# Backward pass of a recurrent-memory attention layer on one core: output gradients by head in column groups, row sums in 32 bit in column groups, turns of 128 columns

## The chip, the cores and the metric

The kernel runs on one core of a Trainium2 chip. The metric is the device time of one execution in microseconds (us), as the median of several runs. A core has TensorE (PE; its loads of the stationary operand are shown as PEld), VectorE (DVE), ScalarE (ACT), GpSimd (POOL) and SyncE (SP), which work beside each other and wait for one another by semaphores. SP and POOL also issue the transfers (DMA). Matmul results lie in PSUM, eight banks of 128 partitions x 512 numbers of 32 bit; operands lie in SBUF.

## The reference

Forward and backward pass of a block: layer norm, attention with a recurrent memory, residual, layer norm, gated feed-forward, residual. S = 2048 rows of D = 448, H = 16 heads of 256, segments of 32 rows, a memory of M = 8 rows. For segment s:

```python
xs = x[:, s * seg_len:(s + 1) * seg_len, :].copy()
h = jnp.concatenate([mem, xs], axis=1)
q = jnp.einsum('btd,dhe->bhte', h, Wq)
...
p = _softmax(scores, axis=-1)
o = jnp.einsum('bhqk,bhke->bhqe', p, v)
o = jnp.einsum('bhte,hed->btd', o, Wo)
mem = o[:, :M, :].copy()
outs.append(o[:, M:, :])
```

The results are the output and, by jax.vjp, the gradients of x, of mem0 and of the seven weights. Since the memory of a segment is the first eight output rows of the segment before it, the 64 segments are a chain: forward from 0 to 63, backward from 63 to 0. A segment works on L = 40 rows, 8 of memory and 32 own ones.

## The kernel before, in words

The program has four stages: `forward_chain` (64 segments), `ffn_phase`, `backward_chain` (64 segments, in tiles of four: tile t = s // 4, place r = s % 4, from r = 3 down to 0) and `tail_phase` (the gradients of the weights, as matmuls over all rows). The kernel is written with a tile scheduler: it orders each engine's instructions by a priority and by its own model of when they are ready, and sets the semaphores. What stands in `with k.prio.crit()` has the highest priority, in the order of the program; `tc.issue_after(ins)` places an instruction behind another of the same engine. Everything outside, such as a tile's closing work, fills gaps. A tile of a pool that is used under one name with few buffers has to wait until the one before it has been read.

A segment of `backward_chain` before the change:

- **Output gradient by weights (L1236).** The gradient of the 40 output rows (`do_roll`: the 32 own rows, and the 8 memory rows that segment s+1 has just written) is multiplied with the output weights: 32 head pieces of 128 x 4 pieces of D, each with 128 x 128 weights as the stationary operand and 40 columns moving. The result, features on partitions, goes to `doT` in four copies.
- **Turns (L1245)** of `doT` in 16 matmuls to rows on partitions (`dO_sb`).
- **Scores (L1254)**: 32 small matmuls with the values give the gradient of the softmax's input, `pD`; DVE makes the score gradient `dS_bd` of it in four operations (L1261 to L1267).
- **Heads (L1213)**: gradients of values (from `dO_sb` and P), of keys (from q and dS) and of queries (from k and the turned dS, L1304). Each set is copied out in own rows (`blk`) and first, memory rows (`lo`), by L75 on DVE and L76 on ACT, the helper `evac`.
- **Rows (L1293)**: 96 matmuls, with 32 columns of `blk` stationary and 448 columns of the turned weights moving. They go to four groups of 32 columns of the array, j % 4, and so to four groups of 32 partitions of one bank, `pH`; the four partial sums still have to be added.
- **Sum and turn (L1319, L1322, L1326)**: `pH` is copied in 32 bit to `om`; four 32-bit matmuls with `om` stationary and `sel` moving (32 columns, which add the four groups) give the sum already turned, features on partitions; DVE copies 8 of its columns to `do_roll` for segment s-1. That closes the chain.
- The own rows' part is kept for the tile (L1334 to L1344), as the gradient of the normed x, turned.

At r = 0 the tile's memory rows are put through the same weights, 96 matmuls (L1378), summed and turned (L1385), turned back in 32 bit (L1393), and the layer norm's backward (`ln_bwd`, L249) writes 128 rows of the gradient of x. This stands outside `crit`.

Queues: SP issues per segment the turned load of the values (L1153, a transfer that transposes) and eight loads of q and k (L1163); per tile the turned load of the output gradient (L1147) and three loads for the norm (L1347, L1349). POOL issues the load of P (L1166) and the stores, and copies in SBUF. Each of these targets has one buffer, so a load waits for its last reader.

The forward chain works on the way from x to q and k in another form, which matters for the prediction: 32 rows stationary, 512 columns of weights moving, in four column groups (L569, and L576 with 64 rows of partitions), then turns of 128 columns (L593).

Of the kernel before, what the change touches and what calls it, by code (L numbers as in the profile page):

```python
# [145 lines left out]
def run_all(k: _K):  # L146
# [15 lines left out]
    psum = ctx.enter_context(tc.tile_pool(name="psum", bufs=1, space=bass.MemoryType.PSUM))  # L162
# [41 lines left out]
    def dt(name, shape, dtype=BF16):  # L204
# [7 lines left out]
              X_o=dt("X_o", [NB, P, MC * P]), HC=dt("HC", [NB * P, DP]), Oh=dt("Oh", [S, D]),  # L212
              DC0=dt("DC0", [P, 4, D]), DC1=dt("DC1", [P, NB - 4, D]))
# [18 lines left out]
    ffn_phase(k, lambda: next(back, None))  # L232
    for _ in back:
        pass
# [3 lines left out]
def cj(j):  # L238
    return (j % 2) * 16 + j // 2
# [869 lines left out]
def backward_chain(k: _K):  # L1109
# [7 lines left out]
    NWIN = 8  # L1117

    WoT_sb = W(0, KC, HD)
# [4 lines left out]
    lo_b = {"v": [A(40, 32, 32), A(42, 32, 32)], "k": [A(44, 32, 32), A(46, 32, 32)], "q": [B(5, 32, 32)]}  # L1124
    dxT = B(7, 1024).bitcast(FP32).rearrange("p (c n) -> p c n", n=P)
    vT = A(49.5, 16, 2 * L)
    dO_sb = A(52, 16, P)
    doT = A(56, 32, 64)
    do_roll = A(60, KC, NWIN, L)
    xn_t = B(9, D)  # L1130
    dh_h = [B(9.875, 448).bitcast(FP32), A(48.5, 448).bitcast(FP32)]
    dx3 = A(48, KC * 48).bitcast(FP32).rearrange("p (c n) -> p c n", c=KC)
    lq3 = k.mv2[:].rearrange("p t n -> p (t n)").bitcast(BF16).rearrange("p (c m) -> p c m", m=M)
    dx2 = [(A(64.5, 96).bitcast(FP32).rearrange("p (c n) -> p c n", c=2), 0, 2, P, 2),
           (A(48.375, 48).bitcast(FP32).rearrange("p (c n) -> p c n", c=1), 2, 3, P, 2),
           (k.maskb[:, 0:24].unsqueeze(1), 3, 4, 64, 2)]
    dx1 = B(4.375, KC * 48).bitcast(FP32).rearrange("p (c n) -> p c n", c=KC)
    dx_stage = [(dx3, 0, KC, P, 3)] + dx2 + [(dx1, 0, KC, P, 1)]
    dhx = A(62.5, KC, P)
    dmr = A(63.5, KC, 16, M)  # L1140
    P_bd, dS_bd, dST_bd = [B(1.25 * i, 8, 2, L) for i in range(3)]
    Pb = [B(3.75, 8, L)]

    def prep_tile(t):
        if t < 0:
            return
        nc.sync.dma_start_transpose(out=dhx, in_=dr["DHb"][t * P:(t + 1) * P, :])  # L1147
        s0 = (4 * t) % NWIN
        for kc in range(KC):
            nc.gpsimd.tensor_copy(out=do_roll[:, kc, s0:s0 + 4, 0:SEG], in_=dhx[:, kc, :].rearrange("p (g j) -> p g j", g=4))  # L1150
# [4 lines left out]
    def load_seg(s):  # L1155
        if s < NSEG - 1:
            load_v(s)
# [6 lines left out]
        P_sb = Pb[0]  # L1164
# [22 lines left out]
    load_seg(NSEG - 1)  # L1187
# [3 lines left out]
    nc.sync.dma_start(out=WoT_sb[:, 0:3, :], in_=dr["To"][:, 0:3, :])  # L1191
    nc.sync.dma_start(out=WoT_sb[0:64, 3, :], in_=dr["To"][0:64, 3, :])
    nc.gpsimd.memset(WoT_sb[64:P, 3, :], 0.0)
# [5 lines left out]
    nc.vector.memset(doT[:, :, L:64], 0.0)  # L1199
    nc.gpsimd.memset(dST_bd, 0.0)  # L1200
    nc.gpsimd.memset(dxT[:, KC - 1, :], 0.0)
    om = k.f32("f1", DP, "omb")
    nc.gpsimd.memset(om[:], 0.0)
# [5 lines left out]
    def head_mm(ps, lhs, rhs_bd, turned):  # L1209
        for cl in range(16):  # L1210
            b, i = divmod(cl, 6)
            at = 8 * (cl // 4 % 2) + 4 * (cl // 8) + cl % 4 if turned else cl
            nc.tensor.matmul(ps[b][:, i * 2 * L:(i + 1) * 2 * L], lhsT=lhs[:, at, :],  # L1213
                             rhs=rhs_bd[:, cl // 2, :, :].rearrange("p g n -> p (g n)"), start=True, stop=True)

    for s in range(NSEG - 1, -1, -1):
# [6 lines left out]
        P_sb = Pb[0]  # L1223
        if r == 2:
            prep_tile(t - 1)
        if s < NSEG - 1:
            load_seg(s)

        with k.prio.crit():
            pss = [k.ps1() for _ in range(4)]  # L1230
            for j in range(MC):
                c = cj(j)
                b, jj = divmod(j, 8)
                for kc in range(KC):
                    with tc.issue_after(k.last_dh.ins) if s == NSEG - 1 and j == 0 and kc == 0 else nullcontext():
                        nc.tensor.matmul(pss[b][:, jj * L:(jj + 1) * L], lhsT=WoT_sb[:, kc, c * P:(c + 1) * P],  # L1236
                                         rhs=do_roll[:, kc, sl, :], start=(kc == 0), stop=(kc == KC - 1))
            for b in range(4):
                k.evac(doT[:, 8 * b:8 * b + 8, 0:L], pss[b][:, 0:8 * L].rearrange("p (c n) -> p c n", n=L), "vsvs"[b])

            def token_major(hf):
                ph = k.ps1()[:].bitcast(BF16)
                for i in range(8):
                    c0 = 2 * (8 * hf + i)
                    nc.tensor.transpose(ph[:, i * P:(i + 1) * P], doT[:, c0:c0 + 2, :].rearrange("p c n -> p (c n)"), ident[:, :])  # L1245
                k.evac(dO_sb[:, 8 * hf:8 * hf + 8, :], ph.rearrange("p (c n) -> p c n", n=P), "sv"[hf])
            token_major(0)
            token_major(1)
            pD = k.ps1()
            for h in range(8):  # L1250
                for g in range(2):
                    for dc in range(DC):
                        j = 2 * (2 * h + dc) + g
                        nc.tensor.matmul(pD[64 * g:64 * g + 64, h * L:(h + 1) * L], lhsT=doT[:, j, :], rhs=vT[:, 2 * h + dc, L * g:L * g + L],  # L1254
                                         start=(dc == 0), stop=(dc == DC - 1), skip_group_check=True)
            if s == 0:
                k.tl.grads(0)
                k.tl.outs(4, 7, 0, 6)
            pD3 = pD[:, 0:8 * L].rearrange("p (h n) -> p h n", n=L)
            prod = k.f32("f2", 8 * L, "prod")[:].rearrange("p (h n) -> p h n", n=L)  # L1260
# [5 lines left out]
            def score_grads():  # L1266
                return nc.vector.tensor_tensor(out=dS_bd, in0=prod.unsqueeze(2).to_broadcast([P, 8, 2, L]), in1=P_bd, op=ALU.mult)  # L1267
            pH = k.po1()
            pps = {}

            def heads(nm, lhs, rhs):
                pps[nm] = [k.ps1() for _ in range(3)]
                head_mm(pps[nm], lhs, rhs, nm != "v")
                for b in range(2 if nm == "k" else 3):
                    own_rows(nm, b, "s" if nm == "v" else "vsv"[b])
                if s == 0:
                    k.tl.outs(*{"v": (7, 9), "k": (9, 10), "q": (10, 11)}[nm], 0, 6)

            def own_rows(nm, b, eng):
                c0, n, v = c12(pps[nm][b], b)  # L1280
                k.evac(blk[nm][:, c0:c0 + n, r * SEG:(r + 1) * SEG], v[:, :, M:L], eng)

            def first_rows(nm, after=None):
                for b in range(3):
                    c0, n, v = c12(pps[nm][b], b)
                    eng = "s" if after is None else "vsv"[b]
# [359 lines left out]
```

## Time and profile before

| | |
|---|---|
| runs | 2926.72, 2932.72, 2935.71 us; median 2932.72 |
| the profiled execution | 2921.87 us, its span 2920.1 us |
| backward segments | from 1257.6 us to about 2252 us of the span |
| granted TensorE clock | 0.995 |
| DMA | 552.14 MB, 743132 packets |

The page gives the busy time of each engine, the chain of work that ended last, and groups of instructions by line. The chain is read as time on the path that sets the end; "issue" in it is time in which nothing that the profile shows was waited for. A group gives its line, engine, output and inputs, its count and its mean time. A matmul's time lasts until its result has landed, so the next one starts earlier than it ends.

### The profile page before, as it was taken

How to read it: one execution, taken by the hardware profiler on the slowest of the kernel's cores; microseconds unless marked ns; L12 is line 12 of the kernel's file. 1: busy time of each engine (PE TensorE's matmuls, PEld its weight loads, DVE VectorE, ACT ScalarE, POOL GpSimd, SP SyncE). 2: the span in 40 equal slices, each digit the busy share in tenths (PEclk: the TensorE clock that was granted, in tenths of full speed). 3: DMA queues.
4: the chain of work that ended last, by engine and by line, in shares of the span. 5: the costliest groups of instructions: out<-in, count | busy, mean ns of one | idle time of the engine just before them, and what ended most of it. 6: DMA issues, size and time to landing. Idle time of an engine off the chain costs nothing.

```text
span 2920.1 us, 108265 instructions
## 1 busy us (share of the span) xinstructions
PE 2805.9 (96%) x47650; PEld 1746.3 (60%) x47650; DVE 1328.6 (45%) x3320; ACT 1077.0 (37%) x2590; POOL 704.1 (24%) x1676
## 2 busy tenths in 40 slices
PE   4999999999999999989999999999999989999998
PEld 3555565555555555667777777677766544545444
DVE  4555565556455666745555555555554011111110
ACT  2554454455454454433333333343333011111110
POOL 1222232233222222422222222222222111212211
PEclk9999999999999999999999999999999999999999
DMA  7577777777778988985555555555555998969941
GB/s 258 152 193 192 192 193 195 192 194 200 198 185 229 285 219 215 257 259 151 142 145 154 144 141 155 137 148 149 142 154 170 347 269 175 207 183 238 207 147 52
DMA packets 743132, 552.14 MB, mean 189 GB/s; under 512 B 601796, under 2 KB 639060, under 8 KB 740100
## 3 DMA queue, kind: packets, MB, share of 16 engines
q1 hardware_dynamic: 692788, 402.38, 55.9%
q0 software_dynamic: 49872, 142.83, 14.4%
q8 instruction: 374, 6.13, 0.9%
q14 instruction: 98, 0.80, 0.1%
HBM read 169.84 MB, written 236.13 MB: 139 GB/s over the span
## 4 chain that ended last, share of the span: by engine, by line
PE 80%; issue 8%; DMA 4%; ACT 3%; DVE 2%; POOL 2%; SPq 0%; POOLq 0%; ACTq 0%; DVEq 0%
PE po L1293 11%; PE psf L1487 8%; PE psf L1236 7%; PE psf L569 6%; PE psf L704 5%; PE psf L1213 5%; PE psf L967 4%; PE po L751 4%; PE fx L1378 3%; PE fx L1487 3%; PE fx L1091 3%; PE psf L593 2%; PE psf L1322 2%; PE psf L1245 2%; PE psf L485 2%
## 5 line engine op out<-in xcount | busy, mean ns | idle before, releaser
L76 ACT CAST arA<-psf 128x384 bf16<-128x384 f32 (+6 forms) x1083 | 419.8, 428 | 845.0 <-PE psf L1487 215.1
L75 DVE CAST arA<-psf 128x256 bf16<-128x256 f32 (+6 forms) x797 | 358.4, 471 | 687.8 <-PE psf L1487 248.9
L1293 PE MATMUL po<-arW,arA 128*32 128x448 bf16 x6144 | 328.1, 355 | 5.6 <-DMA arW<-Tq 4.1
L1487 PEld LDWEIGHTS <-arA 128*128 128x128 bf16 x1440 | 139.0, 98 | 160.6 <-issue 4.8
L1236 PEld LDWEIGHTS <-arW 128*128 128x128 bf16 x8192 | 211.2, 96 | 23.3 <-issue 18.4
L1487 PE MATMUL psf<-arW,arA 128*128 128x512 bf16 x882 | 222.7, 381 | 0.0
L1293 PEld LDWEIGHTS <-arA 128*32 128x32 bf16 x6144 | 146.8, 96 | 120.3 <-ACT arA L76 9.3
L1236 PE MATMUL psf<-arA,arW 128*128 128x40 bf16 x8192 | 217.2, 180 | 0.8 <-DVE arA L1326 0.8
L704 PE MATMUL psf<-arW,arA 128*64 128x512 bf16 x1536 | 212.1, 382 | 0.0
L569 PE MATMUL psf<-arW,arA 128*32 128x512 bf16 x3072 | 189.8, 381 | 7.7 <-DVE arA L75 0.9
L76 ACT COPY arA<-psf 128x512 bf16<-128x512 bf16 (+3 forms) x206 | 142.9, 727 | 39.5 <-PE psf L593 24.0
L76 ACT CAST arB<-psf 128x64 bf16<-128x64 f32 (+1 forms) x320 | 107.7, 337 | 135.1 <-PE psf L576 73.6
L967 PE MATMUL psf<-arW 128*128 128x256 bf16 (+1 forms) x1288 | 149.0, 277 | 5.0 <-DVE arA L75 3.7
L75 DVE COPY arA<-psf 128x512 bf16<-128x512 bf16 (+2 forms) x204 | 104.3, 512 | 99.5 <-PE psf L1245 82.4
L967 PEld LDWEIGHTS <-arW 128*128 128x128 bf16 (+1 forms) x1344 | 103.2, 97 | 56.9 <-issue 45.4
L569 PEld LDWEIGHTS <-arA 128*32 128x32 bf16 x3072 | 70.3, 96 | 105.1 <-issue 28.8
L751 PE MATMUL po<-arW,arA 128*32 128x256 bf16 (+1 forms) x4096 | 126.9, 261 | 1.2 <-DVE arA L75 1.2
L1564 POOL DMA_DIRECT2D out_dram<-arA x96 | 52.2, 544 | 262.0 <-DVE arA L75 233.6
L1527 PE MATMUL psf<-arW 128*128 128x448 bf16 x525 | 111.6, 352 | 3.0 <-DVE arA L75 1.6
L1213 PEld LDWEIGHTS <-arW 128*128 128x128 bf16 x2048 | 79.5, 99 | 49.6 <-issue 48.1
L751 PEld LDWEIGHTS <-arA 128*32 128x32 bf16 x4096 | 104.0, 96 | 8.5 <-DVE arA L75 1.5
L1168 POOL COPY arB<-arB 40x320 bf16<-40x320 bf16 x128 | 58.9, 460 | 174.8 <-DMA arB<-P_all 86.7
(298 smaller groups left out, 4553.5 us busy)
## 6 DMA issues: line engine op xcount, KB each, us to landing
arW<-T SPq DMA_DIRECT2D x256, 128.0 KB
X_o<-arA SPq DMA_DIRECT2D x37, 512.0 KB
T<-arA SPq DMA_DIRECT2D x64, 256.0 KB
X_v<-arA POOLq DMA_DIRECT2D x30, 512.0 KB, 4.9
X_k<-arA POOLq DMA_DIRECT2D x30, 512.0 KB, 4.7
X_q<-arA POOLq DMA_DIRECT2D x30, 512.0 KB, 4.1
out_dram<-arA POOLq DMA_DIRECT2D x84, 128.0 KB, 3.8
VG<-arA SPq DMA_DIRECT2D x64, 160.0 KB
```

Source lines behind the costliest of these rows:

```text
L75: return nc.vector.tensor_copy(out=out, in_=in_)
L76: return nc.scalar.copy(out=out, in_=in_)
L569: nc.tensor.matmul(banks[b][w][32 * q:32 * q + 32, :], lhsT=hT_roll[:, kc, sl, M:L], rhs=(Wq_sb, Wk_sb)[w][:, kc, col(q, b)], start=(b == ...
L704: nc.tensor.matmul(pV[b][64 * g:64 * g + 64, 0:512], lhsT=hT_flat[:, kc, sl * L:sl * L + 64], rhs=Wv_sb[:, kc, n * 512:(n + 1) * 512], sta ...
L751: last = nc.tensor.matmul(pO[32 * q:32 * q + 32, 0:w], lhsT=xblk[:, j, r * SEG:(r + 1) * SEG], rhs=Wo_sb[:, cj(j), 256 * dh:256 * dh + w], ...
L967: nc.tensor.matmul(ps[fp][:, f2 * 256:(f2 + 1) * 256], lhsT=Wt[lo:hi, kc, c * P:(c + 1) * P], rhs=xT[lo:hi, kc, :], start=(kc == 0 and f2 ...
L1091: k.last_dh = nc.tensor.matmul(pdh[:, 0:D], lhsT=srcT[:, tt, c, :], rhs=WT[:, c, :], start=(i == 0), stop=(i == 2 * FC - 1))
L1213: nc.tensor.matmul(ps[b][:, i * 2 * L:(i + 1) * 2 * L], lhsT=lhs[:, at, :], rhs=rhs_bd[:, cl // 2, :, :].rearrange("p g n -> p (g n)"), st ...
L1236: nc.tensor.matmul(pss[b][:, jj * L:(jj + 1) * L], lhsT=WoT_sb[:, kc, c * P:(c + 1) * P], rhs=do_roll[:, kc, sl, :], start=(kc == 0), stop ...
L1293: nc.tensor.matmul(pH[32 * (j % 4):32 * (j % 4) + 32, 0:D], lhsT=blk[nm][:, j, r * SEG:(r + 1) * SEG], rhs=WT[:, cj(j), :], start=(nm == " ...
L1487: k.last_mm = nc.tensor.matmul(pa[i][:, 0:w], lhsT=lhs_of(b)[:, i // 2 * P:(i // 2 + 1) * P], rhs=rhs_of(q, b, i % 2), start=(b == 0), sto ...
L1527: k.last_mm = nc.tensor.matmul(pa[i][:, 0:D], lhsT=lhs_of(b, i), rhs=rhs_of(b), start=(bi == 0), stop=(bi == m + 3))
```

## The change

`backward_chain` gets a new form of the segment. PSUM banks are given by number after the feed-forward stage.

- The own 32 rows of the output gradient are computed with the rows stationary (112 of D's rows at a time, so D = 4 x 112) and 512 columns of weights moving, in four column groups, group q holding heads 4q to 4q+3: 32 matmuls into two banks. The copies (`dO_own`) are the rows by head, and 8 turns of 128 columns make `doT`.
- The 8 first rows, whose gradient is known ahead, are computed for four segments together one tile earlier (`rest_lhs`), turned, kept in `R4_b`, and also written to DRAM (`RO`) and read back by segment (`dOr`).
- The value heads are two sets of 8 matmuls over 160 columns, one for the first rows and one for the own rows, with P loaded once more in two arrangements (`P4`, `P4r`).
- The row sums: `pH` is copied in two halves; four 32-bit matmuls with `sel` stationary add the groups and put 112 columns each on 32 partitions; DVE copies the sum in 16 bit (`ot`), one turn follows, and DVE copies its 8 columns to `do_roll`. The sum also goes through DRAM (`DXQ`, `DXR`), and the layer norm's backward is done two tiles later from there.
- The 96 matmuls of the tile's memory rows (`rest_parts`) are given places by hand.

The diff's core:

```diff
+    DQ = D // 4
+    ot = k.identf[:, 0:DQ // 2].bitcast(BF16)
+    def grads_by_col(lhs, bank, b, c0=0, c1=4):
+        for c in range(c0, c1):
+            for q in range(4):
+                n0 = 1024 * q + 512 * b
+                last = nc.tensor.matmul(bank[32 * q:32 * q + 32, :], lhsT=lhs(c), rhs=WoT_sb[0:DQ, c, n0:n0 + 512],
+                                        start=(c == 0), stop=(c == 3), skip_group_check=True)
+    def grads_turned(bank, src, dst, b, eng="v"):
+        pt = bank[:].bitcast(BF16)
+        for i in range(4):
+            last = nc.tensor.transpose(pt[:, i * P:(i + 1) * P], src[:, i * P:(i + 1) * P], ident[:, :])
+        return last, k.evac(..., pt[:, 0:512].rearrange("p (c x n) -> p x c n", x=2, n=32), eng)
+    def load_rest(s):
+        for w, a, m, n in ((0, 0, 0, 3), (1, 0, 3, 3), (0, 3, 6, 2)):
+            nc.sync.dma_start(out=dOr[32 * w:32 * w + 32, a:a + n]..., in_=src[r][:, :, P * m:P * (m + n)])
+    def load_p(s):
+        for q in range(4):
+            for w in range(2):
+                nc.sync.dma_start(out=P4r[p0:p0 + M, 2 * x + g], in_=pa[64 * g:64 * g + M, x])
+            nc.sync.dma_start(out=P4[32 * q:32 * q + 32, 2 * x + g], in_=pa[64 * g + M:64 * g + L, x])
+    def value_rest(ps):
+        for m in (0, 3, 1, 4, 2, 5, 6, 7):
+            w, a = divmod(m, 3) if m < 6 else (0, m - 3)
+            last = nc.tensor.matmul(v_out(ps, m), lhsT=dOr[32 * w:32 * w + 32, a, :], rhs=p_rows(P4r[32 * w:32 * w + 32], m), ...)
+    def value_own(ps, m0, m1):
+        for m in range(m0, m1):
+            last = nc.tensor.matmul(v_out(ps, m), lhsT=dO_own[:, m * P:(m + 1) * P], rhs=p_rows(P4, m), ...)
+    def summed(ps, part):
+        for q in range(4):
+            last = nc.tensor.matmul(ps[32 * q:32 * q + 32, 0:DQ], lhsT=sel[:], rhs=part[:, DQ * q:DQ * q + DQ],
+                                    start=True, stop=True, skip_group_check=True)
+    V_FILL = {3: 16, 2: 18, 1: 17, 0: 3 * MC}
...
+        if s < NSEG - 1:
+            load_rest(s)
+            load_p(s)
+            load_v(s)
+            load_qk(s)
+            nc.sync.dma_start(out=dr["DXQ"][s + 1], in_=dxs)
+            if r == 3 and t + 2 < NT:
+                nc.sync.dma_start(out=dr["DXR"][t + 2], in_=pxs)
+            if r == 2 and t + 2 < NT:
+                norm_load(t + 2)
+        if r == 3:
             prep_tile(t - 1)
...
-            for j in range(MC):
-                for kc in range(KC):
-                        nc.tensor.matmul(pss[b][:, jj * L:(jj + 1) * L], lhsT=WoT_sb[:, kc, c * P:(c + 1) * P],
-                                         rhs=do_roll[:, kc, sl, :], start=(kc == 0), stop=(kc == KC - 1))
+            for b in range(2):
+                    grads_by_col(lambda c: do_roll[0:DQ, c, sl, M:L], own[b], b)
+            for b in range(2):
+                k.evac(dO_own[:, 512 * b:512 * b + 512], own[b][:], "vs"[b])
+            nc.gpsimd.tensor_copy(out=doT[:, :, 0:M], in_=R4_b[t % 2][:, :, r * M:(r + 1) * M])
+            value_rest(pV)
+            grads_turned(k.bank(0), dO_own[:, 0:512], doT[:, :, M:L], 0)
+            value_own(pV, 0, 4)
+            last_t, turned_v = grads_turned(k.bank(1), dO_own[:, 512:], doT[:, :, M:L], 1)
...
+                last_v = rows_in(pH, lambda j: blk["v"][:, j, r * SEG:(r + 1) * SEG], WvT_sb, ..., start=True)
+            with tc.issue_after(last_v.ins):
+                rest_parts(V_FILL[r])
...
+            nc.vector.tensor_copy(out=om[:, 0:2 * DQ], in_=pH[:, 0:2 * DQ])
+            nc.scalar.copy(out=om[:, 2 * DQ:D], in_=pH[:, 2 * DQ:D])
+            with tc.issue_after(last_r.ins):
+                if r in (2, 1) and t > 0:
+                    last_r = grads_by_col(rest_lhs, pR, 2 - r)
+                elif parts:
+                    last_r = rest_parts(14)
+            with tc.issue_after(last_r.ins):
+                summed(pq, om)
+            nc.vector.tensor_copy(out=ot, in_=pq[:, 0:DQ])
+                nc.tensor.transpose(pm[0:DQ, 0:P], ot, ident[:, :])
+                nc.vector.tensor_copy(out=do_roll[0:DQ, :, (s - 1) % NWIN, SEG:L], in_=...)
+            nc.scalar.copy(out=dxs, in_=pq[:, 0:DQ])
```

## The prediction

> **What bounds the kernel now.** I read the engines' totals first, then the busy time by stretch for the backward stage, then the chain of work that ended last inside one tile of it. The change touches only the backward stage, which runs from about 1257 to 2260 us: 64 segments, one after another, because each needs the memory gradient of the one after it.
>
> ```profile
> PE 2805.9 (96%) x47650; PEld 1746.3 (60%) x47650; DVE 1328.6 (45%) x3320; ACT 1077.0 (37%) x2590; POOL 704.1 (24%) x1676
> ```
> ```profile
> 1588.00:1650.00 62.00, 61.60 (x1492) 44.39 (x1484) 32.47 (x81) 23.86 (x68) 14.08 (x36) 1.00 0.54 145
> ```
> The second line is one tile (four segments): length, then busy PE, PE loads, DVE, ACT, POOL, the granted clock and the DMA share. TensorE is busy for 61.6 of 62.0 us at full clock; nothing else is above 53%. So today the stage is paid for in TensorE time, and the chain names the pieces (start, length, what):
> ```profile
> 1588.25 3.30 PE psf L1236 x128
> 1591.55 0.99 PE psf L1245 x16
> 1592.55 0.62 PE psf L1254 x32
> 1593.16 0.75 PE psf L1213 x16
> 1593.91 0.30 PE fx L1378 x4
> 1594.21 1.60 PE po L1293 x32
> ...
> 1598.28 2.57 PE po L1293 x52
> 1600.85 0.75 PE fx L1378 x13
> 1601.60 1.06 PE psf L1322 x8
> 1602.66 0.49 PE fx L1378 x7
> 1603.15 3.30 PE psf L1236 x128
> ```
> The reader is to see two things. One segment takes 1603.15 - 1588.25 = 14.90 us; the next tile's first L1236 stands at 1650.14, so four take 61.89 us, **15.47 us each** (the fourth holds the tile's closing sums and turns, L1385 and L1393). And the waits at the end (the copy of L1319, the copy of L1326) cost nothing, because the 96 row matmuls L1378 of the previous tile are lying ready: 13 and 7 of them fill the holes.
>
> **What goes, a segment.** L1236: 128 matmuls, 3.30. L1245: 16 turns, 0.99. Value heads (L1213 before L1293): 0.75. L1322: 1.06. Of the tile's end a quarter of L1385 and L1393: (0.44+0.58+0.44+0.37)/4 = 0.46. Together 6.56 us. The rest (scores L1254, 96 rows L1293, 24 rows L1378, heads k and q, L1304) stays: 15.47 - 6.56 = 8.9.
>
> **What comes.** The forward stage already does the first two of these in the new form, so there are rows:
> ```profile
> 414.86 1.48 PE L569 MATMUL psf<-arW,arA 128*32 128x512 bf16 x24
> 416.27 1.26 PE L593 MATMUL psf<-ident,arA 128*128 128x128 bf16 x16
> ```
> - Own gradients: 24 such matmuls take 416.27 - 414.86 = 1.41 us to the next start, 0.059 each; 32 take 1.88. The eight first rows of four segments together take 32 more a tile, 8 a segment: 0.47.
> - Turns: 8 a segment and 8 a tile, 10 at 0.067 (L1245, 16 in 1.07 by starts): 0.67.
> - Value heads: 8 matmuls over 160 columns with 128 rows, and 8 with 32. L1213 gives 0.0425 at 80 columns and L967 0.114 at 256 (49 in 5.60), so 0.07 each by the line between: 0.57 for the first eight. The others have no row: at most the same 0.57; at least half, if the two row groups run side by side as L576 (64 rows, 32 columns: 0.035 against L569's 0.059) suggests. I take 0.45, nearer to L576. Sum 1.0.
> - 32-bit sums, four a segment and four a tile. Nearest row: L1329, 448 columns in 32 bit, two records 0.38 apart, so 112 columns 0.19. Four in turn 0.76, four side by side as L569's groups 0.2. I take 0.4, both ends kept; with the tile's, 0.5.
> - One more turn: 0.07.
>
> Sum 4.6; the work falls from 15.47 to 13.5, about 2 us a segment. **That is not the saving**, because TensorE will have to wait.
>
> **The new path of a segment**, from the moment the memory gradient lies in SBUF. Own gradients 0.04 to 1.92; the last one ends 0.35 later, since a 512-column matmul lasts 0.38. ACT moves the second bank (0.59, L76 at 512): 2.9. Four turns with their latency 0.40, DVE 0.43 (L75, 512 in 16 bit): 3.8. The last 20 score matmuls 0.45: 4.3. DVE's four operations, 1593.21 to 1595.67 in this trace, 2.46: 6.8. In the meantime TensorE has value heads, 32 rows and the 16 to 18 old rows, 0.28+1.6+0.85, so it is occupied but for two holes of 0.1 and 0.35 before the scores. Then dS is turned (0.36), heads k (0.73) cover its copy (0.48), heads q 0.68: 8.6. 64 rows at 0.0475 (L1293: 52 from 1598.21 to 1600.68), with the start of the group 3.1: 11.75, the last ends at 12.1.
>
> Now the end, where the change adds most waits. The sum of the rows is moved out in two halves by DVE and ACT. Both read one bank, and this trace lets two engines read a bank only one after the other:
> ```profile
> ACT arB L1340 <- DVE arA L1326: 66.9, 16, 4.2
> ```
> (who waited for whom, total us, times, longest: L1340 and L1326 only read the same bank). So 0.39 (L264, 224 columns) then 0.35 (between 256 at 0.37 and 96 at 0.24): 12.9, against 0.63 for L1319 in one. The rest gradients (16, 0.9) or 14 old rows lie beside it. The sums end at 13.2 to 13.5, DVE's copy of 112 columns 0.27, the turn 0.22, the copy back 0.19, each with 0.04 of semaphore: 14.05 to 14.3. In these last 0.9 us TensorE has nothing: the next segment's first matmuls are what is waited for, and the value heads behind them need the bank of the sums. Today 7 matmuls of L1378 stand there; they are gone forward into the wait for dS. With the tile's own sums and the small gaps I take **14.4 us a segment** (13.8 to 15.0), 1.07 less than now; 63 times, 67 us.
>
> **A rule that speaks against it.** The chain's rows show a price for a change of shape: 7 L1378 between L1322 and L1236 take 0.49, 0.07 each against 0.0475 inside L1293, so about 0.15 a change. The Trainium skill, "TensorEngine Tiling (Array Packing)", Key Properties, says that a change of tiling mode drains the engine. By that rule the new 32-row matmuls would cost a change more and the sums, now in the mode of the rows, one less: the sum would stay within 0.15 us a segment of what it is without the rule.
>
> **Other engines.** DVE's copies ahead of the scores become 0.69 + 2x0.43 for 2x0.49 + 0.69; it stays near 55%, and the layer norm's part moves into DVE's idle stretch before the copy of the rows. POOL loses the dxT copies and gets the copy of the first rows (about 0.4, L834), with 4 us to spare. SP is another matter, see the second rival.
>
> **The two ends.** At the start the weights are still coming: SP's issue shows it.
> ```profile
> 1254.98 0.32 SPq L1198 DMA_DIRECT2D arW<-Tq  x1
> 1255.42 1.33 SPq L1147 DMA_TRANSPOSE arA<-DHb  x1
> 1262.54 12.95 SPq L1153 DMA_TRANSPOSE arA<-VG  x1
> ```
> Issuing stands still until 1275.5, behind the 3.5 MB loads. Today only q's rows wait there (4.07 us), and the first segment ends at 1281.05. Afterwards its loads of P, the storing of the first rows and their reading back are issued behind the same transfers, so the value heads can start at 1277 to 1280 and 4 to 12 us of the segment are still to come: a loss of 4 to 11, I take 8. At the end the last tiles' norm goes through DRAM, two stores and 22 loads ahead of the tail's loads; today too TensorE reaches full use only at 2263, some 12 us after the last rows. I take 3 (0 to 8).
>
> **The sum.** The profiled execution took 2921.87 (span 2920.1). 67 - 8 - 3 = 56 less gives 2866. The runs shown have their median at 2932.72, 10.85 above the profiled one; the same 56 from there gives **2877**, which I forecast.
>
> **Rivals.**
> 1. The waits eat the gain (chance 0.16). For: every step behind the rows is now serial, and no filler is left. If the sums run in turn, each copy waits for the other engine and each change of shape costs its 0.15, a segment takes 15.1: 0.37 x 63 - 11 = 12 less, **2920**, at the edge of what can be told from no change (0.3%, 8.8 us, is what a measurement of this kernel can tell). Against: the same forward chain (L811 to L813 to L569) shows only 0.02 to 0.04 between steps.
> 2. SP becomes the bound: **slower** (0.20). Now SP issues 9 transfers a segment; then 24 plain ones and one turned, and a tile adds 14 plain and four turns for one: 27.5 plain issues a segment. Undisturbed they follow at 0.37 us (1596.59, 1596.96, 1597.33), 10.2 in all, with 1.34 for V and 0.3 to 1.2 for the turns: 12 to 13 of 14.4, and the stores of dx queue behind a wait for the segment's end, everything later behind them. But L1163's eight take 3.7 to 4.4 us where transfers are in flight, 0.46 to 0.55 each. At 0.50 SP needs 15.7 us: (15.47 - 15.7) x 63 - 11 = 26 more, **2959**. It decides for slower from (15.3 - 1.94)/27.5 = 0.486 an issue, with TensorE then waiting for V or P. Against: 32 and 8 partitions' loads of 320 bytes are small, and loads are ahead by 4 us or more.
> 3. Better than forecast (0.10): the scheduler finds work for the holes and a segment takes 13.6, near the 13.5 of work; 118 - 8 = 110 less, **2823**.
>
> The forecast has the remaining 0.54, with 2833 to 2920 for 15.0 to 13.8 a segment and the ends' bounds (0.47 x 63 - 17 = 13 less; 1.67 x 63 - 5 = 100 less). Faster by over 0.3%: 0.54, 0.10 and over half of rival 1, 0.73; within 0.3%: the rest of rival 1, 0.07; slower: 0.20. The range, 2830 to 2940, leaves out rival 3's better half and nearly all of rival 2.
>
> **What would show it.** Right: first own gradients of successive segments 14.1 to 14.7 us apart; PE busy in the stage down to some 90%, with a hole near 0.9 us ahead of them, released by DVE's copy into the gradient tile; score matmuls released by DVE's turn copy. Wrong: value or score matmuls released by a DMA (rival 2: SP's issues without a gap); sums of 0.76 in turn; the first segment ending past 1293; holes filled by other matmuls (rival 3). The forecast falls if TensorE's waits come from a bank still being read somewhere that I have not put on the path.

## The result and the profile after

The changed kernel takes **3152.68 us** (median of four runs, 3143.33 to 3167.53) against 2934.22 for the kernel before on the same chip: a ratio of **1.0751 [1.0702, 1.0800]**, 7.5% slower. The prediction was 2877, with a range of 2830 to 2940. The profiled execution took 3143.33 (span 3141.1, granted clock 0.948). From the page of the changed kernel, the engines' totals and the chain:

```profile
PE 2805.3 (89%) x41627; PEld 1611.5 (51%) x41631; DVE 1329.4 (42%) x3415; ACT 1032.8 (33%) x2510; POOL 717.3 (23%) x1659
PE 68%; DMA 10%; issue 7%; SPq 7%; ACT 4%; DVE 3%; POOL 1%; POOLq 0%; ACTq 0%; DVEq 0%
```

TensorE has 6000 matmuls fewer and the same busy time; SP's queue and DMA now hold 17% of the chain. The stage by stretch (columns as in the prediction):

```profile
1350.00:2400.00 1050.00, 857.80 (x15657) 507.58 (x15660) 457.26 (x1198) 297.19 (x890) 217.85 (x507) 0.89 0.52 138
```

TensorE is busy 82% of the stage where it was 99%, and the clock is 0.89. **Where the time came from**, by the DVE copy that closes each segment (L1514, before L1326): the first segment ends at 1315.9, before 1280.8 (+35.1); from there to the last one's end 1136.3, before 956.4 (+179.9); the rest +6.0. Sum 221.0, the spans' difference.

Inside the loop the loss is uneven. Between segment ends a typical tile has, for r = 2, 1, 0 and the next tile's r = 3, **16 to 22, 25 to 27.6, 14.74 and 13.97 us**; before, 14.78, 14.88, 14.91, 17.30. I call them first to fourth. (In every fourth tile the third and fourth are longer too, 18 to 19 and 15.5 to 16.6.) The fourth is what the change promised, here in TensorE's main rows:

```profile
1655.43 1.91 PE L1175 MATMUL bank<-arW,arA 112*32 112x512 bf16 x32
...
1658.59 0.94 PE L1416 MATMUL bank<-arA 128*64 128x40 bf16 x32
...
1663.93 3.21 PE L1316 MATMUL bank<-arW,arA 128*32 128x448 bf16 x64
...
1667.64 0.82 PE L1322 MATMUL bank<-om,sel 128*32 128x112 f32 x8
1668.83 0.26 PE L1513 MATMUL bank<-ident,identf 128*112 128x128 bf16 x1 [0.38 <-DVE identf L1510]
```

Own gradients from 0.3 after the old end, scores 3.4, the 64 rows 8.8 to 12, sums to about 13.3, the turn at 13.7: the prediction's path, step for step. The second segment shows what breaks it. SP's rows in the changed kernel (start, length, what it issues) around that segment, which begins at 1613.0:

```profile
1605.67 0.29 SPq L1351 DMA_DIRECT2D om<-DXQ  x1
1612.63 0.34 SPq L1190 DMA_DIRECT2D RO<-arA  x1
1613.02 0.33 SPq L1352 DMA_DIRECT2D om<-DXR  x1
...
1614.85 2.06 SPq L1196 DMA_DIRECT2D arA<-RO  x3
1616.96 0.81 SPq L1204 DMA_DIRECT2D arA<-P_all  x2
...
1621.35 1.32 SPq L1208 DMA_TRANSPOSE arA<-VG  x1
```

SP stands from 1605.96 to 1612.63 in front of the store of the next tile's gradient rows (L1190). Behind it wait the rest of the norm's loads, and behind those every load that the running segment needs: they are issued 1.8 to 13.5 us *after* the segment has begun (V at 8.4, the last load of k at 13.5). The chain of waits in the same stretch:

```profile
1621.00 0.31 SPq L1205
1621.31 0.04 issue
1621.35 5.13 DMA arA<-VG
1626.52 0.57 PE bank L1416 x8
```

V lands 13.5 us after the segment's begin, where the path wanted the scores at 3.4. Over the stage, the waits of SP and of TensorE in the changed kernel (total us, times, longest):

```profile
SPq L1190 <- ACT arB L1519: 91.7, 15, 9.9
SPq L1190 <- ACT arA L76: 32.7, 12, 9.3
...
PE bank L1298 <- DMA arA<-P_all: 134.1, 31, 7.4
PE bank L1416 <- DMA arA<-VG: 28.0, 15, 3.8
```

TensorE's two waits make 162 us. Over the whole loop TensorE stands idle for 198.6 us, where it was 9.8 before. Its busy time is 937.7 us at a clock of 0.89; the last version below does the same work in 870.2 at full clock, so some 65 us (an estimate from these two) are the lower clock. ACT copies the store's data at the end of a segment (here 1612.02 to 1612.61, beside the copy of `dxs` at 1612.70, which is the L1519 that the view names), so the store is late by construction. Adding up the times of SP's own rows from 1400 to 2200 us gives a second reading: **290 us of issuing before, about 620 after** (43 segments, 14.4 us each, in segments that take 18.6 on average), in a queue that, before, waited 350 us for V's buffer.

### The profile page after: what moved, and what is told of

Read it like the earlier page. It is cut to its first block, busy times and chain, and to the rows that moved or that the text cites. A ratio compares the mean times of both kernels' runs of the same rounds, so it can differ in the third digit from the quotient of the medians.

```text
span 3141.1 us, 98056 instructions
## 1 busy us (share of the span) xinstructions
PE 2805.3 (89%) x41627; PEld 1611.5 (51%) x41631; DVE 1329.4 (42%) x3415; ACT 1032.8 (33%) x2510; POOL 717.3 (23%) x1659
## 3 DMA queue, kind: packets, MB, share of 16 engines
q0 software_dynamic: 49872, 142.83, 13.7%
## 4 chain that ended last, share of the span: by engine, by line
PE 68%; DMA 10%; issue 7%; SPq 7%; ACT 4%; DVE 3%; POOL 1%; POOLq 0%; ACTq 0%; DVEq 0%
PE bank L1316 8%; PE psf L1649 8%; PE psf L587 5%; PE bank L1175 5%; PE psf L722 4%; PE psf L985 4%; PE po L769 4%; PE fx L1109 3%; SPq L1204 3%; PE fx L1649 2%; PE bank L1281 2%; PE psf L611 2%; DMA arA<-VG 2%; PE bank L1336 2%; PE bank L1416 2%
## 5 line engine op out<-in xcount | busy, mean ns | idle before, releaser
L75 DVE CAST arA<-psf 128x512 bf16<-128x512 f32 (+2 forms) x285 | 160.1, 562 | 503.0 <-PE psf L1649 249.9
L76 ACT CAST arA<-psf 128x512 bf16<-128x512 f32 (+3 forms) x379 | 190.0, 510 | 532.4 <-PE psf L1649 215.1
L1316 PE MATMUL bank<-arW,arA 128*32 128x448 bf16 x6144 | 333.3, 368 | 0.0
L76 ACT CAST arA<-bank 128x96 bf16<-128x96 f32 (+4 forms) x606 | 192.4, 376 | 204.2 <-PE bank L1304 188.7
L1298 PE MATMUL bank<-arA 32*128 32x160 bf16 x512 | 65.0, 266 | 148.9 <-DMA arA<-P_all 148.1
L1175 PE MATMUL bank<-arW,arA 112*32 112x512 bf16 x2048 | 145.4, 433 | 3.7 <-DVE arA L1514 3.7
L75 DVE CAST arA<-bank 128x384 bf16<-128x384 f32 (+4 forms) x385 | 131.1, 391 | 17.2 <-PE bank L1281 13.1
L1298 PEld LDWEIGHTS <-arA 32*128 32x128 bf16 x512 | 33.4, 101 | 188.1 <-issue 106.5
L75 DVE COPY arA<-bank 128x512 bf16<-128x512 bf16 x143 | 60.8, 425 | 141.2 <-PE bank L1185 137.9
L76 ACT CAST om<-bank 128x512 bf16<-128x512 f32 x65 | 38.1, 586 | 241.9 <-PE bank L1175 217.1
```

The source lines that it names most:

```text
L75: return nc.vector.tensor_copy(out=out, in_=in_)
L76: return nc.scalar.copy(out=out, in_=in_)
L1175: last = nc.tensor.matmul(bank[32 * q:32 * q + 32, :], lhsT=lhs(c), rhs=WoT_sb[0:DQ, c, n0:n0 + 512], start=(c == 0), stop=(c == 3), skip_ ...
L1298: last = nc.tensor.matmul(v_out(ps, m), lhsT=dOr[32 * w:32 * w + 32, a, :], rhs=p_rows(P4r[32 * w:32 * w + 32], m), start=m in (0, 3, 6), ...
L1316: last = nc.tensor.matmul(ps[32 * q:32 * q + 32, 0:D], lhsT=lhs(j), rhs=WT[:, cj(j), :], start=(start and i < 4), stop=(stop and i >= len( ...
```

## The experiments

Theory A: the place of waiting or long issues in SP's one order makes the loads late. Theory B: SP's sum of issues, or the transfers, fill the segment (the first expectations write of the transfers alone). Theory C: the clock. "Loop" is the time from the first to the last segment's end of the profiled run, "start" the first one's end; runs whose time stands without an interval were executed once; edits are to the changed kernel, and where a run builds on another its heading says so; added lines shift the later line numbers by one to five, so a row is read by its operands. Before: start 1280.8, loop 956.4. After: 1315.9, 1136.3.

**The store on POOL**, then the norm's loads (L1351 to L1356) too.

```
-        nc.sync.dma_start(out=dr["RO"][t][:, 512 * b:512 * b + 512], in_=src)
+        nc.gpsimd.dma_start(out=dr["RO"][t][:, 512 * b:512 * b + 512], in_=src)
```

> Only the two stores of the first rows to DRAM per tile are issued from POOL and not from SP; the same bytes move. Theory A (SP issues in order, and the store stands there with a wait of up to 9.9 us ahead of the next segment's loads): the segment at r = 1, now 25 to 27 us, falls to 15 to 17, the one at r = 2 (15 to 22) hardly moves, so about 9 us a tile, 2990 to 3030 in all. Theory B (the transfers themselves are too much or land too late): no change, 3130 to 3160.

3043.97 (loop 1037.0): the second segment falls from 26 to 18 to 22, the first stays. That is A's way, though less than it said (15 to 17); B did not hold.

> As the first, and the eleven loads per tile of the layer norm are issued from POOL as well. Theory A: SP loses 4 us of issuing per tile at r = 2, what is left of the delay at r = 1 goes (14 to 15 us), another 1 to 3 us a tile: 2960 to 3010. Theory B: no change, or slower by what POOL loses to 11 more issues of 0.54 us.

3031.22 (loop 1018.6): the second falls to 14.63, as expected, but the first stays at 16 to 22 and every fourth tile has 22 to 24 in its third: less gain than I wrote.

**One turned load a tile**, from a second copy of the gradient rows, on top of the run before.

```
-        for c in range(4):
-            nc.sync.dma_start_transpose(out=dhx[:, c, :], in_=dr["DHb"][t * P:(t + 1) * P, DQ * c:DQ * c + P])
+        nc.sync.dma_start_transpose(out=dhx, in_=dr["DHc"][t * P:(t + 1) * P, :])
...
+                nc.gpsimd.dma_start(out=dr["DHc"][rows, P * c:P * c + P], in_=dh_b[:, (D // 4) * c:(D // 4) * c + P])
```

> As the second, and the four turned loads of the output gradient per tile become one, from a second copy in DRAM that the feed-forward stage writes with four small stores per tile. Theory A: the four took 5.7 us of SP ahead of the loads of the segment at r = 2; that segment falls from 15 to 22 us to 14 to 16, 3 to 5 us a tile less than the second kernel: 2890 to 2950. Theory B: no change against the second kernel.

2974.84 (loop 952.5, start 1328.2): most tiles 56 to 62, four 67 to 74, where POOL's store waits in turn (70.6 us for ACT's copies). Worse than expected, by the start and by those tiles.

**Fewer P loads**: `load_p(s)` is left out in all segments but the first, so P is stale and the value gradients are not the reference's.

```
             load_rest(s)
-            load_p(s)
             load_v(s)
```

> The twelve loads of P in two arrangements per segment are left out but for the first segment (the value gradients are computed with a stale P); everything else as changed. Theory A: SP has 12 issues of 0.35 us less a segment, so loads stand 4 us earlier in every segment, and what the store's wait and the four turned loads cost falls by up to 4 us each: r = 2 to 14 to 17, r = 1 to 21 to 23, 3000 to 3070. Theory B: the 61 KB less per segment are a small part of the volume, under 20 us less.

2995.93 (loop 990.1): the first segment falls to 14.15, the second stays at 20 to 22. Twelve issues fewer help one place, and the store still holds the other. The written B (under 20 us) fell. The run takes away issues and bytes together, so it does not tell a shorter sum of issues from earlier places.

**The store on ACT's queue**, then with the one turned load, then with the memory rows' four turns as one.

```
-        nc.sync.dma_start(out=dr["RO"][t][:, 512 * b:512 * b + 512], in_=src)
+        nc.scalar.dma_start(out=dr["RO"][t][:, 512 * b:512 * b + 512], in_=src)
...
-            for c in range(4):
-                nc.sync.dma_start_transpose(out=rows[:, DQ * c:DQ * c + DQ], in_=dmr[0:DQ, c].rearrange("p s m -> p (s m)"))
+            nc.sync.dma_start_transpose(out=rows[:, 0:D].rearrange("p (c d) -> p c d", d=DQ), in_=dmr[0:DQ].rearrange("p c s m -> p (c s m)"))
```

> The two stores of the first rows per tile, and the two ahead of the first segment, are issued from ACT, which writes what they store, so no other queue has to wait for them. Theory A (order of issue on SP): r = 1 falls as with POOL to 18 to 20 us, no new waits on POOL; at the start, SP no longer holds the loads of the last two weights until 1282 us, and the first segment ends 10 to 20 us earlier than the 1315.9 of the changed kernel: 3000 to 3035. Theory B (volume): no change, 3130 to 3160.

> As the fifth, and one turned load of the output gradient per tile in place of four (from a second copy in DRAM); the norm's loads and all loads of P stay on SP. Theory A: a tile takes 57 to 60 us in nearly all tiles (56.7 undisturbed) against 61.9 before; with a start that is 15 to 25 us later than before the change and an end that is 7 later, 2890 to 2930. Theory B: no better than the third kernel, 2975.

> As the sixth, and the four turns of the memory rows once in four tiles become one transfer. Theory A: the tiles with a segment of 20 to 23 us (every fourth) lose 4 to 7 us each, 10 to 25 us in all against the sixth. Theory B: no change against the sixth.

3103.99, 3047.79 and 3033.82 (loops 1098.8, 1019.7, 1012.6). The first two miss by far: the second segment stays at 22 to 24.5. (The third's own effect came in every fourth tile, whose third segment falls from 19 or 20 to 15 or 16; the -14 in all, of which 7 are in the loop, is no more than one kernel's runs differ by.) SP's rows in the last of the three, and its wait there:

```profile
1646.43 2.25 SPq L1197 DMA_DIRECT2D arA<-RO  x3
1652.63 0.66 SPq L1205 DMA_DIRECT2D arA<-P_all  x2
```
```profile
SPq L1205 <- DMA RO<-arA: 57.0, 13, 6.0
```

The loads of P stand 4 us on for a store that another engine issued and whose data they do not use. The semaphore numbers in the trace say why. All transfers that SP and ACT issue share eight semaphores, which are handed out in turn, and an issue first waits until the last transfer with its own number has landed. (Where SP alone issues, as in the changed kernel, each number comes back with every eighth transfer, 1348 times of 1348 from 1350 to 2200 us.) Here ACT issued the store at 1650.88 with number 104; it landed at 1652.61, and the P load at 1652.63 is the next with number 104. All 13 of these waits are of this kind, and 14 more, 28.1 us, of the store of `dxs`. So ACT's queue does not take a store out of SP's order. POOL's transfers have eight semaphores of their own, and the store on POOL gave a loop of 1037.0 against 1098.8.

**The store behind its segment's loads**, on SP.

```
+                with tc.issue_after(k.last_load.ins):
+                    rest_saved(t - 1, 1 - r, rO)
```

> The changed kernel with one edit in the order alone: the RO store in the loop stays on SP, but is placed behind the q and k loads of its own segment, not ahead of that segment's loads. Same transfers, same queue, same number of SP issues. Theory A (the place of a waiting store in SP's one order delays the loads that follow): the second segment of a tile falls from 26 us to 15 to 20, the first (behind the four turned loads) stays at 17 to 22, the loop loses 16 x 7 to 10 us; 3010 to 3045 us in all. Theory B (SP has more issues than the segment has time for, or the transfers themselves are too much): no change within 20 us of 3150. If the move of the store to another queue was what helped (RO from POOL gave 3044, from ACT 3104), this run must be no better than 3104.

3047.20 (loop 1043.2): one line of order, same transfers, same queue, -96 against the profiled run of the changed kernel; the second segment 18 to 21, a little above what I wrote. TensorE's waits from 1350 us on fall from 134.1 to 59.0 us for P and from 28.0 to 13.4 for V. Theory A is shown for this store. The next two add to it the single turned loads as above, and then the norm's loads on POOL (`nc.gpsimd` for `nc.sync` in `norm_load`).

> As the run before it, and the four turned loads of the next tile's gradient rows as one (from a second copy in DRAM, written by four small POOL stores a tile in the feed-forward stage), and the memory rows' four turns as one. Theory A: first segment 14.1 to 15, second 15 to 17 (eleven norm loads still ahead of its loads), third 14.7, fourth 14.0, so 58 to 61 us a tile against 61.9 before the change; with a start some 35 to 45 us late (the four extra stores a tile too) and an end 6 late: 2900 to 2945. Theory B: no better than the 2975 that the same with the RO stores and norm loads on POOL gave.

> As the run before it, with the eleven norm loads a tile issued by POOL. If these eleven hold the second segment's loads: it falls to 14.1 to 15 us, 57 to 59 a tile, 10 to 35 us less than the run before. If POOL's slower issues are in the way of its own copies instead (the run with both on POOL showed waits of POOL behind its stores), the second segment falls but single tiles of 66 us and more come back, and the sum is no better.

2995.28 (loop 977.3) and 2954.04 (931.3). In the first the first segment falls to 14.1 in most tiles and the second stays at 18 to 23, above my figure; 2995 is no better than 2975, which I had written as B's sign. This step takes issues away as well as moving them, so it does not part A from B. With the norm's eleven loads away from SP the second is 14.65 in most tiles, but single tiles still have 15 to 23 somewhere. The loop is now 25 us shorter than before the change; the start (1324.2) eats it.

**The start freed**, on the run before: the buffer `om` shares with an earlier store, the first RO stores stand behind the load of Tq, one DHc store a tile.

```
-            dh_t = k.f32(("f3", "f1")[tt], (D, DP)[tt], "dh_t")[:, 0:D]
+            dh_t = k.f32(("f1", "f3")[tt], (DP, D)[tt], "dh_t")[:, 0:D]
...
+            with tc.issue_after(last_w.ins):
+                rest_saved(NT - 1, b, src)
```

> As the run before it (2954.0; loop 931.3 us between the first and the last segment's end, first segment's end at 1324.2), with three edits at the start of the stage and none in the loop: the gradient buffer om shares its place with the f1 use of the feed-forward's first tile of a group and not its second, so that it comes free one store earlier; the first two RO stores stand behind the load of Tq on SP, and not ahead of the loads of Tk and Tq; the second copy of the gradient rows is one store a tile of 128 columns each and not four. Theory A (what made the start late is again loads and stores that wait in one order, behind a store that is itself late): the first segment ends at 1285 to 1300, the loop stays at 925 to 935, 2915 to 2930 in all. Rival (the start is late for its own matmuls, turns and small loads): still 1310 or later, 2940 or more.

2933.53 (0.9982 [0.9963, 1.0002] of before; start 1310.9, loop 927.3): the start came 13.3 us earlier, where I wrote 24 to 39; at 1310.9 it stands where the rival put it. In the changed kernel ACT's rows at the start show what was freed:

```profile
1281.07 0.59 ACT L76 CAST om<-bank 128x512 bf16<-128x512 f32 x1 [15.26 <-DMA DH<-dh_t]
```

In this run the wait has moved on: the RO store issued at 1270.34 lands at 1290.8, after the weights' loads that were issued before it (the last at 1288.1), and DVE can write `om` again only at 1290.9.

**Tq behind the first read of RO; the turned load behind V; four P loads on ACT.**

```
+            if r == 2:
+                with tc.issue_after(k.last_v.ins):
+                    prep_tile(t - 1)
...
-                nc.sync.dma_start(out=P4r[p0:p0 + M, 2 * x + g], in_=pa[64 * g:64 * g + M, x])
+                (nc.sync, nc.scalar)[w].dma_start(out=P4r[p0:p0 + M, 2 * x + g], in_=pa[64 * g:64 * g + M, x])
...
+    with tc.issue_after(first_rest.ins):
+        nc.sync.dma_start(out=WqT_sb, in_=dr["Tq"])
```

> As the run before it (2931.9 span; tiles of 56.1 to 65.3 us, the first segment of a tile 14.1 to 20.2), with three edits that show in different places. (a) The turned load of the next tile's gradient rows stands behind the load of V of a tile's first segment, and not ahead of that segment's loads: if the place in the order is what costs, the first segment falls to 14.1 to 15 in every tile (loop 927 to about 895 to 905 us). (b) Four of the twelve P loads of a segment are issued by ACT: if SP's sum of issues (some 25 in 14 us, without a gap in the trace) is what leaves segments of 15 to 17 us elsewhere, they fall to 14.0 to 14.8; if ACT's own copies are put back by it, the fourth segment, now 13.97, gets longer. (c) Tq is loaded behind the first RO stores and their read: the read lands some 15 us sooner, and the first segment ends at 1292 to 1302 and not at 1311. In all 2885 to 2910; if all three are wrong, 2930 or more.

2973.18 (1.0121 [1.0083, 1.0160]; start 1298.8, loop 984.8). The start came as written; the loop became worse, and SP's waits name it: `L1218 <- DMA arW<-T`, 81 times in 850 us, q and k loads waiting for other loads of q and k. These too are waits for a load's own semaphore number: with ACT's four P loads in the ring of eight they make 208 us from 1300 to 2260, against 59 in the run before. Two edits lay in the loop, so the next runs take them apart (all P loads on SP again; then `prep_tile` back at its old place), and add or leave out four issues:

```
                 nc.sync.dma_start(out=P4r[p0:p0 + M, 2 * x + g], in_=pa[64 * g:64 * g + M, x])
+                if w and s < NSEG - 1:
+                    nc.sync.dma_start(out=P4r[p0:p0 + M, 2 * x + g], in_=pa[64 * g:64 * g + M, x])
```
```
+                if w and s < NSEG - 1:
+                    continue
                 nc.sync.dma_start(out=P4r[p0:p0 + M, 2 * x + g], in_=pa[64 * g:64 * g + M, x])
```

> As the run before it without its edit (b): all P loads are issued by SP again; the turned load of the next tile behind V's, and Tq behind the first read of RO, stay. If ACT's P loads made the loop 985 us and not 927: it comes back. If the turned load's place is what lengthens a tile's first segment (14.1 to 20.2 in the run with the place before): 14.1 to 15.5, a tile 58, the loop 895 to 912, the first segment's end at about 1299: 2885 to 2908. If the turned load only pushes something else: 925 or more in the loop, 2915 or more.

> Only edit (c), Tq behind the first read of RO, on the kernel of the run with the freed start (2933.5; loop 927.3, first segment's end 1310.9): the loop as there within 10 us, the first segment's end at 1297 to 1301, 2916 to 2930. The difference of this run and the one beside it is the place of the turned load alone.

> As the run beside it, with four of the twelve P loads of every segment issued twice by SP (the same rows to the same place; 4 more issues of 0.35 us and 20 KB more traffic). If SP's sum of issues fills the segment, as the trace with no gap in its queue suggests (25 issues and their waits in 14 us): every segment of 14.0 to 14.7 becomes 15.4 or more, the loop 60 to 100 us longer, 2980 to 3020. If there is room in SP's order and only the late places cost: 0 to 20 us more.

> As the run with edit (c) only, without four of the twelve P loads of a segment (the second copy of the memory rows' P keeps the first segment's values, so the value gradients are not the reference's; no other work is left out). If SP's sum is what is left above 57.4 us a tile: all segments but the first of a tile 14.0 to 14.8, first 14.1 to 16, the loop 895 to 908, 2885 to 2905. If the turned load's place alone is left: the first segment stays at 14.1 to 20, the loop within 10 us of the run beside it.

| run | time | start | loop | SP's rows in 1400 to 2200 |
|---|---|---|---|---|
| turned load behind V | **2917.80**, 0.9943 [0.9921, 0.9965] | 1304.2 | 916.1 | 680 |
| turned load before the loads | 2932.05, 0.9988 [0.9972, 1.0004] | 1306.6 | 932.5 | 674 (53 segments, 12.7 each) |
| the same, 4 more P loads | 3015.61 | 1304.1 | 1017.8 | 662 |
| the same, 4 fewer | 2905.94 | 1303.8 | 910.2 | 627 |

The first two rows are the runs that take the edits apart. With (b) undone the loop comes back, so ACT's P loads had cost 68.7 us. The place of one turned load is worth 16 us of loop, 14 of the medians (first segment 14.1 to 15.8 against 14.1 to 20.3); 916.1 lies just above the 895 to 912 that I wrote, and 2917.80 above its 2908. Edit (c) alone brings the start to 1304 to 1307, not to 1301 or less. Four issues more cost 85.3 us in the loop's 62 segments, **1.38 a segment, 0.34 an issue**, about the length of one issue. This is not wholly clean: SP also waits 20.4 us in the stage for the first of the two copies to land, and the loss is uneven (second segments take about 14.9, fourth ones 14.4 to 20.7, where I wrote 15.4 or more for all). Four fewer give 22.3, and two tiles in three then take 56.2 to 58.9 us. TensorE's waits for loads, with four fewer and with four more issues (13.6 for P and 9.9 for V with neither), agree:

```profile
PE bank L1303 <- DMA arA<-P_all: 4.3, 3, 1.6
```
```profile
PE bank L1303 <- DMA arA<-P_all: 32.4, 26, 4.0
...
PE bank L1422 <- DMA arA<-VG: 14.7, 7, 3.0
```

The first row of this table is a version that beats both kernels; it is 0.57% (0.35 to 0.79) faster than the kernel before. Its stage by stretch:

```profile
1350.00:2200.00 850.00, 810.07 (x15940) 488.89 (x15932) 464.22 (x1213) 301.64 (x905) 304.47 (x663) 1.00 0.65 173
```

TensorE is back at 95% and full clock, and the DMA share is 0.65 against 0.52 in the changed kernel: the volume of the transfers was not the limit.

## Why the prediction was wrong

- **The path of a segment was right.** 14.4 (13.8 to 15.0) was forecast; undisturbed segments take 13.97 to 14.74, and a tile without a late load 57.4 us (in several of the later versions), 14.35 a segment. Whether a change of mode has a price cannot be told from this: by the prediction the rule moves a segment by 0.15 us at most. (The line from L1213 to L967 gives 0.075 and not 0.07 for 160 columns, 0.03 us a segment.)
- **The step that failed is the second rival's price, and the sentence set against it.** The forecast has no term for a late load; in the loop TensorE stood idle for 198.6 us, 162 of them for P and V, and a segment took 18.3 us on average and not 14.4. Two of the signs named for being wrong came: value and score matmuls released by a DMA, and a first segment that ends past 1293. The rival's 2959 was far too small as well. Its "12 to 13 of 14.4" was 14.4 us of SP's rows a segment. The load of the first rows' gradient takes 0.68 an issue where I counted 0.37 (three a segment), V 1.55 instead of 1.34, the tile's turns 1.48 a segment and not 0.3 to 1.2; the memory rows' four turns, 0.47 a segment, were not counted; P (0.34 to 0.39) and q, k (0.37) were right. So the deciding point of 0.486 an issue, which sets SP's sum against the length of a segment, was the wrong test: by these rows the 27.5 issues took about 0.40 each, below it, and the kernel was slower all the same.
- **"Loads are ahead by 4 us or more" failed most.** Before, V's load waited 350 us in all for its buffer: SP had slack, and I read it as lead. In the changed kernel each of the added loads has one buffer, which the running segment lets go, so SP has to do its round in the segment itself, and a store that waits for the end of the segment before stands in front of it (up to 9.9 us). I wrote of the stores of dx that they queue "behind a wait for the segment's end, everything later behind them", and put no price to it; the store that stood was that of the first rows, and moving it is worth 93 us of the loop (1136.3 to 1043.2).
- **The start was mis-sized:** 4 to 11 forecast, 35.1 measured, the first end far past 1293. I counted the loads behind the weights, and missed that `om` waits for the feed-forward's last DH store (15.26 us in ACT's row above) and that the loads of Tk and Tq stood behind the RO store that needs it. Freed, the start still costs 18 to 26.
- **The end:** 0 to 8 forecast, 6.0 measured; TensorE waits 5.0 us for X_o, whose load stands behind the last norm's loads on SP.
- **Theory C** is a follower: the clock falls after a wait has begun, and adds to it. In the long second segment the clock by stretch is

```profile
1616.00:1621.30 5.30, 0.30 (x4) 0.13 (x3) 2.01 (x7) 1.18 (x3) 0.00 (x0) 0.76 0.33 106
1621.30:1626.50 5.20, 1.56 (x12) 1.05 (x13) 0.00 (x0) 0.62 (x2) 0.00 (x0) 0.50 0.57 135
...
1629.00:1632.00 3.00, 3.00 (x37) 1.27 (x40) 1.76 (x3) 0.82 (x4) 0.87 (x2) 0.50 0.23 53
1632.00:1636.00 4.00, 4.00 (x93) 2.62 (x89) 2.36 (x8) 1.66 (x5) 1.06 (x3) 0.94 0.42 145
```

after the idle stretch it is 0.50 until 1632; from 1626.5 on that is 5.5 us of TensorE work at half speed, some 2.7 us on top of the wait, as an estimate. Own gradients behind another such wait (1580.24) took 3.53 us for 1.9. The Trainium skill, "TensorE: Matmul & The Clock Gate", Part 1: The HAM clock gate, gives half the clock after an idle window of about 3.4 us. These rows agree: the clock halves at 1618.79 and is full again at 1632.44, and the trace's stretches of one clock here last 1, 2, 4, 5 or more times 3.41 us. Where the loads come in time it is 1.00.

The Trainium skill, "DMA: Bandwidth & Descriptors", Issuing engines are not separate DMA queues, says that starting transfers on several engines saves only the sequencer's time, usually small against the transfer. For one transfer that is so here (V: 1.32 us of issuing, landed 5.13 us after its start). The sum is another matter: 12.7 us of issuing a segment, and four small issues more lengthen the loop by 85.3 us. Nor was SP's time simply saved by issuing from ACT: the store there gave 37.5 us of the loop where POOL gave 99.3, and four P loads there cost 68.7, by the shared semaphores.

**Still open:** how much of the last versions' SP time is the sum of issues and how much waits for landings and buffers; and what is left of the start.

## What to carry to other kernels

Price an added transfer on the queue that issues it, in order: what it waits for, and which loads stand behind it; a store of a segment's last result belongs behind the next loads, not ahead. A queue's sum counts from the moment its buffers come free, not as a mean over the segment: 12.7 us of issuing in segments of 15.1 us left no room for four issues more. Test it by doubling a few issues: if each costs its own length, the queue is close to the bound. And look at the semaphore numbers: a transfer can wait for one that only shares its number.

## What the runs showed of the hardware

- A plain issue on SP mostly takes 0.30 to 0.40 us, one with 32 partitions of strided rows (L1196) 0.68 with its gap, a turned one 1.2 to 1.6; V's 160 KB landed 5.1 us after its issue.
- In this program's traces SP and ACT share eight semaphores for their transfers and POOL has eight others; an issue waits for the landing of the last transfer with its number (1650.88, 1652.61 and 1652.63 above).
- The 32-bit sums of a segment leave eight records; four of them, one half of the rows, take 0.39 us with their latency (2450.54), and the first half lies beside the copy of the second.
- Two engines read one bank in turn, as forecast: 0.39 on DVE from 1667.19, then 0.35 on ACT from 1667.67, after a wait for DVE's semaphore. Whether they could read it together, no run shows.
